# Lightning attention and a leaky-ReLU MLP on one core: a new order of units, conversions and loads, and five constants of the planner

## The chip, the core and the metric

The kernel runs on one core of a Trainium2 chip. The metric is the device time of one execution in microseconds (us), lower is better. The kernel before took 597.89 us, the median of three runs (597.32 to 598.83). A separate execution was profiled; its times are the ones in the profile.

The core has five engines with queues of their own, which run side by side and wait for each other by semaphores: TensorE (PE: matrix products and transposes), VectorE (DVE), ScalarE (ACT), GpSimd (POOL) and SyncE (SP), which here only issues transfers between DRAM and the on-chip memory. Each engine executes its queue strictly in the order in which it was written. So an order of the program is an order of five queues.

## The reference

Attention with decay over four batches, eight heads, 768 positions and 64 features, in blocks of 64, with a running state per head; then a two-layer MLP on the 3072 tokens with weights in double precision.

```python
for b in range(nb):                                  # nb = 12 blocks of 64
    intra = np.einsum('bhic,bhjc->bhij', qb, kb) * Dmask[None]
    intra = np.einsum('bhij,bhjd->bhid', intra, vb)
    inter = np.einsum('bhid,bhde->bhie', qb * lam_pow[None], kv_state)
    out[:, :, sl] = intra + inter
    kb_dec = kb * rev_pow[None]
    kv_state = lam_block[None, :, None, None] * kv_state + np.einsum('bhsd,bhse->bhde', kb_dec, vb)
...
x = np.ascontiguousarray(attn_out.transpose(0, 2, 1, 3)).reshape(B * S, H * D)   # [3072, 512]
h = x @ w_in                                         # [512, 2048], float64
g = np.maximum(0.01 * h, h)
return (g @ w_out).astype(np.float32)                # [2048, 512], float64
```

## The kernel before

**Precision.** Every operand of the two large products is held as three parts, h, l and m, made from a float32 value: h is a rounded copy (ACT), l the remainder against h, m a combination of both (DVE). A product is three matmuls, one for each part, that PE adds up in PSUM. So each operand costs one ACT and two DVE instructions before PE can use it, and they come in that order: h, l, m.

**Tiles.** The 3072 tokens are 24 chunks of 128; four chunks are a group of 512 tokens, so there are six groups, 0 to 5. The 2048 columns of the first product are eight pairs (0 to 7) of 256 columns.

**The up stage, to about 345 us.** A round `r c` does the attention of chunk c and ends with the three parts of x for that chunk (L533 xh on ACT, L534 xl on DVE, then xm). In its middle PE must not go on before a copy of two columns, L517, has read the result of the first half; the planner puts that copy on DVE or on ACT. `up(g, p)` is the first product of group g with pair p: for each half of the columns, four steps of PE (h, l, an ACT pass over the bank at L786, m), and an ACT evacuation with the leaky ReLU at L791. Three PSUM banks, b10, b11 and b2, are used in turn. The result goes to DRAM, plain (`G`) or as sums and differences of its quarters (`BB`, made by `sums` on DVE). `up(1, 5, 0, 3)` is the first three chunks of a group and `up(1, 5, 3, 4)` the last one. `ORDER` lists in which order the pairs come in groups 2 to 4; group 5 takes them from 0 to 7.

**Conversions.** `wi p` loads pair p of the first weight matrix as float64 (L611), splits it into float32 with bit operations on ACT (L614, L616, L618) and DVE (L620, L621), and then makes its parts: the head wh on ACT (L627) or DVE (L629), as the planner chooses, wl on DVE (L632), wm on DVE (L647). `wo p h` converts half a pair of the second matrix and stores it in DRAM. `wp p` (`w_out_parts`) loads it again and makes its three parts in place of the first matrix's: L627 or L629, L632, then L640 (DVE) and L642 (ACT). `ws p` (`w_sums`) makes the sums of quarters of a pair that the Strassen-like units need: a load, four DVE subtractions or additions, and parts as before. `wq p` (`w_apart`, its head L699) does this for pairs 4 and 5 and sends the parts to DRAM; `wd` (`fetches`) fetches them back.

**The down stage, from about 345 us.** Three parts, in the order 0, 2, 1; part pr covers groups 2 pr and 2 pr + 1. Pairs below `NSP = [2, 6, 4]` are multiplied by a Strassen scheme with seven units t = 1 to 7 for each two pairs: `s(t, u)`, 12 matmuls of 128x512 (L909). The other pairs are plain units `n(p, gi)`, 24 matmuls each; the last of a part, written `l`, also turns its results (`turn_out`, DVE L1003) and stores them (`store_out`). Each unit is made ready by `unit`:

```python
add("DMA", UNIT_DMA, go, keys, wr("m"))      # SP: load of 512 KB into part m of a ring slot
add("ACT", 1.05, head, kg, wr("h"))          # L882: h
add("DVE", 1.25, low, kg + [f"rh{j}"], wr("l"))              # L885: l
add("DVE", 1.25, middle, [f"rh{j}", f"rl{j}"], [f"rm{j}"])   # L889: m
```

There are five ring slots, taken in turn in the order in which the units are written, so the load of a unit waits until PE has finished the unit five places before. Where a needed block was not stored, the load is of two blocks (L899) and DVE subtracts them first (L901). The results gather in four pairs of banks, X, Z, Y and V. `copy Z X` and `copy Y Z` (`copy_banks`, L1022, two ACT copies) and `add Y V` and `add V Z` (`add_banks`, L1027 on ACT, L1028 on DVE) move them on at set points; the units write X, V, Z, X, Z, Y, Z for t = 1, 5, 6, 2, 7, 3, 4. The kernel ends with `ending`, two plain units in pieces with their stores.

**What sets the order.** `seq` is a list of such steps, written out by hand. Each step's instructions are given to `Plan` with a length, what they read and write, and a rank: their place in `seq`, less a lead. `emit` then plays the five engines forward with these lengths: again and again the operation that can start first is taken, and among equals the one with the lowest rank. The lengths (`UNIT_DMA = 1.7` for a unit's load, for instance) are the planner's own. They decide nothing but the order of the five queues. `LEAD` (8 places; `LEAD0` for part 0) is the lead of a unit's load, head, l and m, and of copies and additions between banks; `WPR` and `WSR` shift `wp` and `ws` behind their place. After a store that ACT issues, an entry of length 0.55 without an instruction stands in the planner's DMA queue.

Of the kernel before, what the change touches and what calls it, by code (L numbers as in the profile page):

```python
# [166 lines left out]
def kernel(  # L167
# [21 lines left out]
    NG = NCH // GC  # L189
# [13 lines left out]
    NS, NS0 = 4, 2  # L203
    NSP = [2, 6, 4]
    WS0, WS1 = 1, 2
    LEAD = 8.0
    TURN_B = 2
    HOLD, WPR, WSR, LEAD0 = 0.0, 4.0, 2.0, 8.0
    WSLACK = 5.0
    DV = 10  # L210
    QSL = 1.0
    RUNS = {10: (-8.0, 0.8), 12: (4.0, 0.0)}
    C4 = P // 4
    UNIT_DMA, UNIT_SLACK = 1.7, -0.5
    HALF = (slice(0, D), slice(D, 2 * D))
    assert NCB % TURN == 0 and D == 64 and KO == HP == 4 and SEQ % C == 0 and NCH % GC == 0 and d_model == T == 512 and NP % 4 == 0

# [19 lines left out]
    X = [[sb([P, KO, T], f"x{x}{i}", F32R) for x in "hlm"] for i in range(2)]  # L237
# [54 lines left out]
    add = plan.add  # L292
# [713 lines left out]
    def store_out(pr, gi, m, cs, queues):  # L1006
        t0, n, w = (2 * pr + m) * T + gi * HT, HT // C4, len(cs) * C4

        def store(a, q):
            c0 = a * P + cs[0] * C4  # L1010
            q.dma_start(out=out[t0:t0 + HT, c0:c0 + w].rearrange("(b i) j -> i b j", i=C4),
                        in_=otile[a * C4:(a + 1) * C4, m * n:(m + 1) * n, cs[0]:cs[-1] + 1, :].rearrange("i b c j -> i b (c j)"))

        for a, x in enumerate(queues):
            e, q = {"S": ("DMA", nc.sync), "A": ("ACT", nc.scalar)}[x]
            add(e, 0.5, lambda a=a, q=q: store(a, q), [f"o{c}{m}" for c in cs], [f"out{pr}{gi}{m}{a}{cs[0]}"], rank=6.0 if len(cs) == 4 else -1.5)
            if x == "A":
                add("DMA", 0.55, lambda: None, [f"o{c}{m}" for c in cs] + [f"out{pr}{gi}{m}{a}{cs[0]}"], [], rank=6.0 if len(cs) == 4 else -1.5)

    def copy_banks(d, s):  # L1020
        for i in range(2):
            add("ACT", 0.6, lambda i=i: nc.scalar.copy(acc[d][i], acc[s][i]), [ACC[s][i]], [ACC[d][i]], rank=-LEAD)  # L1022

    def add_banks(d, s):
        for i in range(2):
# [3 lines left out]

    seq = [  # L1030
# [5 lines left out]
    nxt, n_out, begin = 3 * GC, 0, len(seq)  # L1036
    ORDER = [2, 1, 4, 3, 0, 5, 7, 6]
    steps = [(g, p) for g in range(2, NG) for p in (ORDER if g < NG - 1 else range(NP))]

    def key_of(g, p):  # L1040
# [16 lines left out]
    for pr, before in ((0, None), (2, 0), (1, 2)):  # L1057
        def s(t, u):
            return "s", pr, t, u

        def n(p, gi, r=pr):
            return ("n", r, p, gi) if p < NP - 1 else ("l", r, p, gi, (0, 1, 2, 3) if gi == 0 else (2, 3, 0, 1))

        late = [n(p, 1, before) for p in range(NS, NP)] if pr else []
        if pr:
            if pr == 2:
                seq += [
                    s(1, 0), s(1, 1), ("copy", "Z", "X"), late[2], late[0], s(6, 1), late[1], ("wq", 4), late[3], s(6, 0),
                    ("copy", "Y", "Z"), s(5, 0), s(5, 1), s(7, 1), ("add", "Y", "V"), s(7, 0), ("add", "V", "Z"), s(2, 1),
                    n(4, 0), s(2, 0), n(6, 0), s(4, 1), n(5, 0), s(4, 0), s(3, 1), s(3, 0), n(7, 0), ("wq", 5)]  # L1070
            else:
                seq += [
                    late[1], late[0], s(1, 0), s(1, 2), s(1, 1), ("wd", 0), late[2], ("copy", "Z", "X"), s(2, 0), s(6, 2),
                    late[3], s(2, 1), ("wd", 2), s(5, 0), s(5, 1), s(6, 0), s(6, 1), ("copy", "Y", "Z"), s(5, 2), s(7, 0),
                    s(2, 2), s(7, 2), ("wd", 1), s(7, 1), ("add", "Y", "V"), ("add", "V", "Z"), s(3, 2), s(4, 0), s(4, 2),
                    s(4, 1), n(6, 0), n(7, 0), s(3, 0), s(3, 1)]
        else:
            def put(x, *new):
                i = seq.index(x)
                seq[i:i] = new  # L1080

            put(("up", NG - 1, 4), ("ws", 0))
            put(("up", NG - 1, 5), ("ws", 1))
            put(("up", NG - 1, 7), ("fr",))
            put(("up", NG - 1, 7), s(1, 0), ("copy", "Z", "X"))
            seq += [
                s(6, 0), s(5, 0), ("copy", "Y", "Z"), s(7, 0), ("add", "Y", "V"), ("add", "V", "Z"), n(2, 0), n(2, 1), n(3, 1),
                s(4, 0), n(3, 0), s(2, 0), n(6, 0), n(5, 0), n(4, 0), ("ws", 2), s(3, 0), ("ws", 3), n(7, 0)]
    seq += [n(p, 1) for p in range(NSP[1], NP - 2)] + [("end", 1, 1, NP - 2)]

    freed = False
    for n, x in enumerate(seq):
# [37 lines left out]
        elif x[0] == "s":  # L1130
            strassen(*x[1:], LEAD if x[1] else LEAD0)
        elif x[0] == "n":
# [40 lines left out]
```

## Time and profile before

| what | value |
|---|---|
| three runs | 597.32, 597.89, 598.83 us |
| the profiled execution, its own time | 598.96 us |
| its span, from the first to the last instruction | 597.2 us |
| POOL: rounds' state products and loads, none after some 270 us | 134.8 us busy |
| granted TensorE clock | 9 or more tenths in all 40 slices of the span |
| mean rate of the transfers | 224 GB/s, 133.55 MB |
| load of a Strassen unit (`xm<-b`, 35 of 512 KB) | median 4.3 us from issue to landing |
| load of a plain unit (`xm<-g`, 17 of 512 KB) | median 4.3 us |
| load of half a pair of `w_in`, of `w_out` (16 each, 512 KB) | 5.2 us, 5.0 us |
| head of a unit, L882 on ACT | 51 times, mean 1062 ns |
| l of a unit, L885 on DVE | 51 times, mean 1219 ns |
| m of a unit, L889 on DVE | 52 times, mean 1225 ns |
| pass over a bank, L786 on ACT | 97 times, mean 582 ns |

The page counts an engine as busy while one of its instructions runs. The line of a group of instructions names the line of the kernel, the engine, the operation and its tiles (out<-in), how many there are, the busy time and the mean of one, and behind the last bar the idle time just before them with what ended it. The list of waits has, for each engine and place, the engine and the operation that ended the wait, then the time waited, the number of waits, and the longest. The chain of waits is followed back from the last instruction, at each step to what released it. In the timeline an instruction's line has its start, its length, its engine and line, the operation, and in square brackets how long the engine had been idle before it and which instruction ended that.

### The profile page before, as it was taken

To read this page: it belongs to the slowest core of one execution; us is meant where nothing else is said; L and a number is where in the kernel's file an instruction comes from. 1 tells how busy PE (TensorE), PEld (TensorE's weight loads), DVE (VectorE), ACT (ScalarE), POOL (GpSimd) and SP (SyncE) were. 2 spreads that over 40 slices of the span, in tenths; PEclk is the share of its full clock that TensorE was granted. 3 is DMA by queue.
4 is the path that set the end of the run, shared out by engine and by line. 5 is a ranking of instruction groups with operands and counts; after the bars stand their busy time and mean duration, and the time that the engine had idled before them with its cause. 6 is when DMAs were issued, how large, how long until landed. Compare 5 with 4: busy or idle time off the path is not lost.

```text
span 597.2 us, 13439 instructions
## 1 busy us (share of the span) xinstructions
PE 584.0 (98%) x5324; PEld 481.7 (81%) x5324; DVE 433.4 (73%) x596; ACT 306.2 (51%) x478; POOL 134.8 (23%) x170
## 2 busy tenths in 40 slices
PE   7899999999999999999999999999999999999997
PEld 5678888888888888888788878888888888888886
DVE  5899986525677464675269989886698887788972
ACT  4688883445555555565588783433343332335410
POOL 2654494616436436431000000000000000000000
PEclk9999999999999999999999999999999999999999
DMA  8899766978989989997889765534868668869644
GB/s 208 224 292 250 239 175 156 228 206 211 264 240 269 242 268 254 261 294 225 260 265 300 239 201 185 187 124 154 236 200 253 195 218 251 281 201 294 186 121 88
DMA packets 171199, 133.55 MB, mean 224 GB/s; under 512 B 101376, under 2 KB 147200, under 8 KB 171136
## 3 DMA queue, kind: packets, MB, share of 16 engines
q1 hardware_dynamic: 155376, 123.24, 70.8%
q10 hardware_dynamic: 13200, 5.77, 3.7%
q0 software_dynamic: 2560, 3.68, 2.4%
q8 instruction: 42, 0.69, 0.5%
q14 instruction: 21, 0.17, 0.1%
HBM read 85.99 MB, written 46.66 MB: 222 GB/s over the span
## 4 chain that ended last, share of the span: by engine, by line
PE 90%; DVE 5%; DMA 2%; ACT 1%; issue 0%; POOL 0%; SPq 0%
PE b L767 42%; PE po L909 13%; PE b L909 12%; PE psc L909 11%; PE pt L909 4%; PE po L339 3%; PE psc L339 3%; DMA attb<-in_q_dram 2%; DVE w L620 1%; DVE wm L647 1%; DVE w L621 1%; DMA attb<-in_k_dram 1%; PE pt L429 1%; DVE wl L632 0%; PE po L429 0%
## 5 line engine op out<-in xcount | busy, mean ns | idle before, releaser
L767 PE MATMUL b<-xh,wh 128*128 128x512 f32 (+2 forms) x392 | 103.5, 387 | 0.9 <-ACT xh L533 0.8
L767 PE MATMUL b<-xl,wl 128*128 128x512 f32 (+2 forms) x392 | 103.4, 387 | 0.7 <-DVE xl L534 0.6
L767 PE MATMUL b<-xm,wm 128*128 128x512 f32 (+2 forms) x392 | 103.9, 393 | 0.0
L882 ACT ACTIVATE xh<-xm 128x1024 fp32r<-128x1024 f32 x51 | 54.1, 1062 | 82.8 <-DMA xm<-b 50.3
L767 PEld LDWEIGHTS b<-xh,wh 128*128 128x128 f32 x392 | 72.8, 188 | 16.8 <-ACT xh L533 0.9
L767 PEld LDWEIGHTS b<-xl,wl 128*128 128x128 f32 x392 | 72.8, 188 | 15.9 <-DVE xl L534 1.0
L767 PEld LDWEIGHTS b<-xm,wm 128*128 128x128 f32 x392 | 71.3, 188 | 14.8
L786 ACT ACTIVATE b<-b 128x512 f32<-128x512 f32 (+2 forms) x97 | 56.2, 582 | 49.0 <-PE b L767 48.5
L791 ACT ACTIVATE gs<-b 128x512 f32<-128x512 f32 (+2 forms) x97 | 57.1, 593 | 44.0 <-PE b L767 38.2
L885 DVE SCALAR_TENSOR_TENSOR xl<-xm,xh 128x1024 fp32r<-128x1024 f32 x51 | 62.2, 1219 | 16.2 <-ACT xh L882 15.8
L889 DVE SCALAR_TENSOR_TENSOR xm<-xl,xh 128x1024 fp32r<-128x1024 f32 x52 | 63.7, 1225 | 4.0
L478 DVE TENSOR_TENSOR att<-psc,att 128x512 f32<-128x512 f32 x24 | 16.5, 688 | 38.9 <-PE psc L339 38.9
L488 POOL TENSOR_TENSOR att<-att 128x256 f32<-128x256 f32 x40 | 33.9, 847 | 42.2 <-DVE att L485 41.3
L400 POOL DMA_DIRECT2D attb<-in_q_dram x64 | 39.4, 622 | 4.9 <-DVE att L409 4.3
L449 POOL TENSOR_TENSOR att<-att 128x512 f32<-128x512 f32 (+1 forms) x20 | 24.8, 1240 | 53.7 <-PE po L339 18.9
L445 POOL TENSOR_TENSOR attb<-attb,att 128x512 f32<-128x512 f32 (+1 forms) x23 | 27.7, 1202 | 37.4 <-DMA attb<-in_k_dram 16.3
L909 PE MATMUL psc<-xm,wm 128*128 128x512 f32 x80 | 31.2, 391 | 0.8 <-DVE xm L889 0.8
L621 DVE CUSTOM_DVE_ANT_0 w<-w,lows 128x1024 uint16<-128x1024 uint16 x32 | 26.3, 822 | 7.3 <-ACT lows L618 5.9
L909 PE MATMUL psc<-xl,wl 128*128 128x512 f32 x80 | 31.2, 390 | 0.0
L909 PE MATMUL psc<-xh,wh 128*128 128x512 f32 x80 | 31.1, 389 | 0.0
L620 DVE TENSOR_SCALAR w<-w 128x512 int32<-128x512 int32 x32 | 22.1, 692 | 8.7 <-ACT w L614 8.5
L616 ACT ACTIVATE lows<-raws 128x512 uint16<-128x512 uint32 x32 | 25.2, 786 | 1.1 <-DVE w L621 1.1
(189 smaller groups left out, 1102.6 us busy)
## 6 DMA issues: line engine op xcount, KB each, us to landing
xm<-b SPq DMA_DIRECT2D x35, 512.0 KB, 4.3
b<-gs SPq DMA_DIRECT2D x24, 512.0 KB, 3.7
g<-gs SPq DMA_DIRECT2D x23, 512.0 KB, 3.6
xm<-g SPq DMA_DIRECT2D x17, 512.0 KB, 4.3
raws<-in_moe_w_in_dram SPq DMA_DIRECT2D x16, 512.0 KB, 5.2
raws<-in_moe_w_out_dram SPq DMA_DIRECT2D x16, 512.0 KB, 5.0
attb<-in_k_dram SPq DMA_DIRECT2D x48, 128.0 KB, 4.2
attb<-in_v_dram SPq DMA_DIRECT2D x24, 256.0 KB, 4.5
```

What stands on the lines that cost most here:

```text
L339: nc.tensor.matmul(dst[HALF[cols]], lhsT=lhsT[HALF[rows]], rhs=rhs[HALF[rows]], start=start, stop=True, skip_group_check=True)
L400: (move if nm == "k" else carry)(0.55 if nm == "k" else QSL, lambda o=o, z=z, e=nc.sync if nm == "k" else nc.gpsimd: e.dma_start(out=o.rea ...
L488: add("POOL", 0.7, lambda new=new, j=j: nc.gpsimd.tensor_tensor(state[(j + 1) % 4], new, _bc(lam_c, 2, D), op=ALU.mult), [f"st{j % 4}", "f ...
L620: add("DVE", 0.42, lambda: nc.vector.tensor_scalar(d, d, 3, None, op0=ALU.logical_shift_left), [], [key])
L621: add("DVE", 1.0, lambda: nc.vector.tensor_tensor(d, d, low, op=ALU.add), [kl], [key])
L767: nc.tensor.matmul(dst, lhsT=w[z][:, kk * 2 * P + f * P:kk * 2 * P + (f + 1) * P], rhs=x[z][:, kk, toks], start=start and kk == 0, stop=kk ...
L786: add("ACT", ns, lambda b=b: nc.scalar.activation(out=b, in_=b, func=AF.Copy, bias=0.0, scale=S + 1.0), [], [kb], rank=-1.5)
L791: add("ACT", t, lambda o=o, x=s_: nc.scalar.activation(out=o, in_=x, func=AF.Prelu, bias=0.0, scale=(1.0 + 1.0 / S) / (WS * U), alpha=0.01 ...
L882: nc.scalar.activation(out=ring[j][0], in_=g(), func=AF.Copy, bias=0.0, scale=NEAR)
L885: nc.vector.scalar_tensor_tensor(ring[j][1], g(), 1.0, ring[j][0].bitcast(F32), op0=ALU.mult, op1=ALU.subtract)
L889: nc.vector.scalar_tensor_tensor(m, l.bitcast(F32), -S, h.bitcast(F32), op0=ALU.mult, op1=ALU.add)
L909: nc.tensor.matmul(dst, lhsT=lhs(z), rhs=ring[j][z][:, col:col + n], start=first and z == 0, stop=z == 2, skip_group_check=True)
```

## The change

The operations stay as they are: the same loads, products and stores are written, with the same lengths and tiles, but for two small choices between DVE and ACT that the planner makes (one more instruction on ACT, one fewer on DVE). What is new is their order, by four kinds of edits.

- Constants: `LEAD` 8 to 12, `WPR` 4 to 3, `LEAD0` 8 to 4, `UNIT_DMA` 1.7 to 1.85, and the entry behind ACT's stores 0.55 to 0.45.
- The head of `seq`, from its third row: which pairs are multiplied with groups 0 and 1, where the rounds 6 to 11 stand between them, and when the conversions 3, 4, 7, 0 and 1 come. The first chunks of `up(1, 5)` move behind `up(0, 4)`, and `r 7` stands ahead of `wi 4`.
- `ORDER` for groups 2 to 4 becomes 1, 6, 0, 3, 2, 5, 7, 4.
- The three parts of the down stage. In part 0 the sums `ws 0` and `ws 1` are put before `up(5, 1)` and `up(5, 3)`, the first Strassen unit and the copy behind it before `up(5, 5)`, unit s(5,0) before s(6,0), and n(6,0) is the first plain unit in place of n(2,0). In the other two parts the plain units that are left from the part before (`late`), the Strassen units and the copies and additions stand in another order. In part 1, in PE's queue as the planner writes it, unit l(7,1) (`late[3]`, four pieces of six matmuls) stood before the change with its first piece behind s(1,2), s(1,1), n(6,1) and s(2,0) and the rest behind s(6,2); now its first two pieces stand behind s(1,2), s(1,1) and n(4,1) and the other two behind s(6,2) and s(6,0). Its ring slot is that of s(1,2) in both.

```diff
--- before.py
+++ after.py
@@ -203,15 +203,15 @@
     NS, NS0 = 4, 2
     NSP = [2, 6, 4]
     WS0, WS1 = 1, 2
-    LEAD = 8.0
+    LEAD = 12.0
     TURN_B = 2
-    HOLD, WPR, WSR, LEAD0 = 0.0, 4.0, 2.0, 8.0
+    HOLD, WPR, WSR, LEAD0 = 0.0, 3.0, 2.0, 4.0
     WSLACK = 5.0
     DV = 10
     QSL = 1.0
     RUNS = {10: (-8.0, 0.8), 12: (4.0, 0.0)}
     C4 = P // 4
-    UNIT_DMA, UNIT_SLACK = 1.7, -0.5
+    UNIT_DMA, UNIT_SLACK = 1.85, -0.5
     HALF = (slice(0, D), slice(D, 2 * D))
     assert NCB % TURN == 0 and D == 64 and KO == HP == 4 and SEQ % C == 0 and NCH % GC == 0 and d_model == T == 512 and NP % 4 == 0
 
@@ -1015,7 +1015,7 @@
             e, q = {"S": ("DMA", nc.sync), "A": ("ACT", nc.scalar)}[x]
             add(e, 0.5, lambda a=a, q=q: store(a, q), [f"o{c}{m}" for c in cs], [f"out{pr}{gi}{m}{a}{cs[0]}"], rank=6.0 if len(cs) == 4 else -1.5)
             if x == "A":
-                add("DMA", 0.55, lambda: None, [f"o{c}{m}" for c in cs] + [f"out{pr}{gi}{m}{a}{cs[0]}"], [], rank=6.0 if len(cs) == 4 else -1.5)
+                add("DMA", 0.45, lambda: None, [f"o{c}{m}" for c in cs] + [f"out{pr}{gi}{m}{a}{cs[0]}"], [], rank=6.0 if len(cs) == 4 else -1.5)
 
     def copy_banks(d, s):
         for i in range(2):
@@ -1029,12 +1029,12 @@
 
     seq = [
            ("a", 0), ("a", 1), ("a", 2), ("a", 3), ("wi", 5), ("b", 4), ("up", 0, 5), ("wi", 2), ("wi", 6), ("r", 4), ("r", 5),
-           ("up", 0, 2), ("up", 0, 6), ("wi", 3), ("up", 0, 3), ("r", 6), ("wi", 4), ("up", 1, 5, 0, 3), ("wi", 7),
-           ("up", 0, 4), ("r", 7), ("up", 0, 7), ("wi", 0), ("up", 1, 3), ("wi", 1), ("up", 0, 1), ("ls",), ("up", 0, 0),
-           ("lt",), ("up", 1, 0), ("r", 8), ("r", 9), ("up", 1, 7), ("up", 1, 4), ("up", 1, 6), ("r", 10), ("r", 11),
-           ("up", 1, 2), ("up", 1, 1), ("up", 1, 5, 3, 4)]
+           ("up", 0, 2), ("wi", 3), ("r", 6), ("up", 0, 6), ("up", 0, 3), ("r", 7), ("wi", 4), ("up", 0, 4), ("wi", 7),
+           ("up", 1, 5, 0, 3), ("up", 1, 4), ("wi", 0), ("wi", 1), ("ls",), ("up", 0, 7), ("up", 0, 0), ("up", 0, 1), ("lt",),
+           ("up", 1, 7), ("r", 8), ("r", 9), ("up", 1, 0), ("up", 1, 3), ("r", 10), ("up", 1, 6), ("r", 11),
+           ("up", 1, 5, 3, 4), ("up", 1, 1), ("up", 1, 2)]
     nxt, n_out, begin = 3 * GC, 0, len(seq)
-    ORDER = [2, 1, 4, 3, 0, 5, 7, 6]
+    ORDER = [1, 6, 0, 3, 2, 5, 7, 4]
     steps = [(g, p) for g in range(2, NG) for p in (ORDER if g < NG - 1 else range(NP))]
 
     def key_of(g, p):
@@ -1065,27 +1065,27 @@
         if pr:
             if pr == 2:
                 seq += [
-                    s(1, 0), s(1, 1), ("copy", "Z", "X"), late[2], late[0], s(6, 1), late[1], ("wq", 4), late[3], s(6, 0),
-                    ("copy", "Y", "Z"), s(5, 0), s(5, 1), s(7, 1), ("add", "Y", "V"), s(7, 0), ("add", "V", "Z"), s(2, 1),
-                    n(4, 0), s(2, 0), n(6, 0), s(4, 1), n(5, 0), s(4, 0), s(3, 1), s(3, 0), n(7, 0), ("wq", 5)]
+                    s(1, 0), late[0], late[1], s(1, 1), ("copy", "Z", "X"), late[2], ("wq", 4), late[3], s(6, 0), s(5, 0),
+                    s(6, 1), s(5, 1), ("copy", "Y", "Z"), s(7, 0), s(7, 1), ("add", "Y", "V"), ("add", "V", "Z"), s(3, 0),
+                    n(4, 0), s(2, 0), n(6, 0), s(4, 1), n(5, 0), s(3, 1), s(4, 0), s(2, 1), n(7, 0), ("wq", 5)]
             else:
                 seq += [
-                    late[1], late[0], s(1, 0), s(1, 2), s(1, 1), ("wd", 0), late[2], ("copy", "Z", "X"), s(2, 0), s(6, 2),
-                    late[3], s(2, 1), ("wd", 2), s(5, 0), s(5, 1), s(6, 0), s(6, 1), ("copy", "Y", "Z"), s(5, 2), s(7, 0),
-                    s(2, 2), s(7, 2), ("wd", 1), s(7, 1), ("add", "Y", "V"), ("add", "V", "Z"), s(3, 2), s(4, 0), s(4, 2),
-                    s(4, 1), n(6, 0), n(7, 0), s(3, 0), s(3, 1)]
+                    late[1], s(1, 0), late[2], s(1, 2), s(1, 1), late[0], ("wd", 0), ("copy", "Z", "X"), s(6, 2), s(6, 0),
+                    ("wd", 2), late[3], s(6, 1), s(5, 0), ("copy", "Y", "Z"), s(5, 2), s(5, 1), ("add", "Y", "V"), s(7, 2),
+                    ("wd", 1), s(7, 0), s(2, 0), s(2, 2), s(2, 1), s(7, 1), s(3, 1), ("add", "V", "Z"), s(4, 0), s(4, 1),
+                    s(4, 2), n(6, 0), n(7, 0), s(3, 0), s(3, 2)]
         else:
             def put(x, *new):
                 i = seq.index(x)
                 seq[i:i] = new
 
-            put(("up", NG - 1, 4), ("ws", 0))
-            put(("up", NG - 1, 5), ("ws", 1))
+            put(("up", NG - 1, 1), ("ws", 0))
+            put(("up", NG - 1, 3), ("ws", 1))
             put(("up", NG - 1, 7), ("fr",))
-            put(("up", NG - 1, 7), s(1, 0), ("copy", "Z", "X"))
+            put(("up", NG - 1, 5), s(1, 0), ("copy", "Z", "X"))
             seq += [
-                s(6, 0), s(5, 0), ("copy", "Y", "Z"), s(7, 0), ("add", "Y", "V"), ("add", "V", "Z"), n(2, 0), n(2, 1), n(3, 1),
-                s(4, 0), n(3, 0), s(2, 0), n(6, 0), n(5, 0), n(4, 0), ("ws", 2), s(3, 0), ("ws", 3), n(7, 0)]
+                s(5, 0), s(6, 0), ("copy", "Y", "Z"), s(7, 0), ("add", "Y", "V"), ("add", "V", "Z"), n(6, 0), n(5, 0), n(2, 0),
+                s(4, 0), n(3, 0), n(2, 1), s(2, 0), n(3, 1), s(3, 0), n(4, 0), n(7, 0), ("ws", 2), ("ws", 3)]
     seq += [n(p, 1) for p in range(NSP[1], NP - 2)] + [("end", 1, 1, NP - 2)]
 
     freed = False
```

`late` is `[n(4, 1), n(5, 1), n(6, 1), l(7, 1)]` of the part before, `put(x, ...)` inserts steps ahead of step x, and ("end", 1, 1, 6) is the call of `ending`.

## The prediction

> **What bounds the kernel now.** I read the engines' busy times first, then TensorE's own waits, then the places of those waits in the order of time.
>
> ```profile
> span 597.2 us, 13439 instructions
> ...
> PE 584.0 (98%) x5324; PEld 481.7 (81%) x5324; DVE 433.4 (73%) x596; ACT 306.2 (51%) x478; POOL 134.8 (23%) x170
> ...
> PE 90%; DVE 5%; DMA 2%; ACT 1%; issue 0%; POOL 0%; SPq 0%
> ```
>
> TensorE (PE) is busy for 98% and makes 90% of the chain. An edit of order alone leaves its 3822 issued matmuls and transposes as they are, and the 30 fillers (L286) stand in the same places in both orders, so the change can only take away or add waits of PE. These are PE's waits from 62 us on, where the two orders part (up to 62 us all five queues agree, apart from two evacuations and one small copy):
>
> ```profile
> PE psc L909 <- DVE xm L889: 0.8, 1, 0.8
> PE b L767 <- DVE xl L534: 0.6, 1, 0.6
> PE po L339 <- DVE att L517: 0.3, 1, 0.3
> PE po L339 <- ACT att L517: 0.3, 1, 0.3
> ```
>
> That is 2.0 us in all. The chain around the largest one shows that it is longer than its 0.8:
>
> ```profile
> 353.15 0.98 ACT wm L642
> 354.13 0.96 ACT w L1027 x2
> 355.09 0.97 ACT xh L882
> 356.06 0.02 issue
> 356.08 1.24 DVE xl L885
> 357.32 0.02 issue
> 357.34 1.24 DVE xm L889
> 358.58 0.04 issue
> 358.62 1.21 PE psc L909 x4
> ```
>
> The first product of unit n(2,0) starts at 356.93; its third, due two products (2 x 0.227) later at 357.38, starts at 358.62: 1.24 us are lost. So PE's losses after 62 us come to 0.64 + 0.34 + 0.28 + 1.24 = 2.50 us. That is the most that the change can win; what it can lose has no such bound.
>
> **The change, part by part.** Unit lengths below are from the timeline of PE: a product of 128x512 every 0.227 us, so an s unit (12) 2.72 and an n unit (24) 5.44; a block of four in the up stage 0.907. A place in the new order is the old place of a common neighbour plus such lengths.
>
> *First units (seq, up to unit r 7).* The old order puts up(1,5) on three chunks behind up(0,3), and its second block waits:
>
> ```profile
> 65.89 0.97 PE L767 MATMUL b<-xl,wl 128*128 128x384 f32 x4 [0.64 <-DVE xl L534]
> ...
> 77.23 0.46 PE L339 MATMUL po<-att 64*64 64x64 f32 x16 [0.34 <-DVE att L517]
> ```
>
> DVE was late with xl there because it made wh of pair 4 first (L629, 62.97 to 64.63). In the new order up(0,4) comes first; its wh moves to ACT (L627, 1.06 in its rows), and a two-column copy (L517) moves from ACT to DVE, behind an L620 that ended at 62.10. That copy releases the last products of chunk 6: it ended at 61.93 and would now end at 62.10 + 0.15 = 62.25. PE took up those products at about 62.1, so 0.15 us are added. Then: L621 ends at 62.25 + 0.69 = 62.94, wh on ACT at 62.94 + 1.06 = 64.0, wl (L632) at 64.0 + 0.05 + 1.22 = 65.27. PE starts xh of up(0,4) at 64.38 + 0.15 = 64.53 and wants wl at 65.44: no wait. With the 1.39 that L632 took at 55.22, beside POOL, it would be 65.44 too; I add 0.1 for the uncertainty. Both sides: 0 if all fits, 0.64 if the same tightness returns.
>
> The second wait (0.34) came from the same small copy behind L620 (75.82 to 77.10). In the new order r 7 comes 4 us earlier (69.9), and ahead of the copy stand wm of pair 4 and four conversions of pair 7: 68.5 + 0.85 + 0.69 + 0.42 + 0.69 = 71.1, while PE reaches the point at 69.9 + 0.9 + 0.7 = 71.5. No wait; if I am wrong, 0.34. Sum of this part: -0.64 - 0.34 + 0.15 + 0.1 = -0.73.
>
> The Trainium skill, "GPSIMD Engine Reference", section "Specifications", says that GpSimd shares its SBUF interfaces with VectorE and that they contend when a VectorE instruction has two SBUF inputs. L632 has two, and POOL's state product (L488) would run beside it at 64.1; the rows differ (1.22 beside POOL at 66.80, 1.39 at 55.22), and what POOL lost is clearer (1.54 against 0.62 alone). By the rule alone wl could be late by some tenths, and the sum would be -0.6 in place of -0.73.
>
> *Order of the up units, 78 to 325 us.* ORDER and seq change which pair is next, not how much. PE had one wait there (0.28 at 295, before a copy on ACT that stays). The rounds r 9 to r 23 fall within 1.3 us of their old places, so their loads have the same time. Cover: ACT 10 to 12 us and DVE 8 to 14 of every 20. A bank that is evacuated one instruction late would cost one L786, 0.58. I take 0.
>
> *Turn from up to down, 325 to 365 us.* Now s(1,0) stands before up(5,5), 5.5 us earlier, s(5,0) before s(6,0), and the weight sums of pair 1 ahead of three conversions. DVE is busy 18.8 of 20 us here and ACT 15.6. Laying the new DVE queue end to end from 296.5 (conversions L632, L640 1.23 each, sums 0.42, unit steps 1.22) I get s(5,0) ready at 338.7 for its start at 347.7, s(6,0) at 344.4 for 351.3 and s(7,0) at 349.4 for 354.0. The thinnest cover is ACT's evacuation of the banks of up(5,6) and up(5,7): 0.4 to 0.9 us. I cost these moves at 0; without cover each costs its overshoot, at most the one head (L882, 1.05) that now stands ahead of an evacuation.
>
> What remains is the wait of the first n unit, now n(6,0). Its head waits on ACT for two bank copies, that can start only when the banks of s(6,0) are written. In the old order the two copies before the head (L1027) began as s(5,0) ended. Same chain: from the end of s(6,0) (354.03) minus 0.15, copies 0.94, head 1.06, DVE 2 x 1.25 = 358.4. PE is there after s(7,0), 354.03 + 2.72, and wants the third product at 357.2: 1.2 late, as before (1.24). So this, the largest wait, is kept. Both sides: 0 (all 1.24 won) if ACT gets the head in before the copies' end; 2.3 if wm of pair 7 (1.06 on ACT) slips behind the copies.
>
> *Down stage, parts 0 and 2.* The order of n units changes; they give slack (5.44 of PE against 2.45 of DVE each). The run of s units after the second l unit grows from six to seven; with two bank copies, four turn_outs (0.7) and w_apart's 4 x 0.42 + 2.45 placed earlier, the thinnest unit, s(6,1), is ready 0.9 us ahead of PE (the old run's thinnest had 1.8). Cost 0.
>
> *Down stage, part 1.* Each unit's load waits for a ring slot, that is for the PE end of the unit five places before in the order of loads.
>
> ```profile
> 508.30 0.53 SPq L879 DMA_DIRECT2D raws<-g  x1
> ...
> 514.71 1.22 DVE L885 SCALAR_TENSOR_TENSOR raws<-raws 128x1024 fp32r<-128x1024 f32 x1 [0.39 <-ACT raws L882]
> 516.04 1.23 DVE L889 SCALAR_TENSOR_TENSOR raws<-raws 128x1024 fp32r<-128x1024 f32 x1
> ```
>
> This is unit l(7,1): slot free as s(1,2) ends at 508.10, load landed at 513.54 (5.24), head 1.06, ready at 517.26, 9.16 after the slot. In the old order 10.88 us of PE (s, n, s) lie between and PE comes at 518.98. In the new one only s(1,1) and n(4,1), 8.16, as PE takes half of l(7,1) before s(6,2). Its third product is due 8.16 + 0.45 = 8.61 after the slot: 0.55 late with this landing, 0.4 early with the 4.3 that is the median of these loads. I take +0.2 (a landing of 4.85, between the two). Behind it the run of s units has more room than before (1.6 us at the thinnest, against 0.49 for s(4,2)), which wins nothing, as there was no wait. The last units and stores are the same.
>
> The constants (LEAD, WPR, LEAD0, UNIT_DMA, 0.45) only rank the queues that are counted above. One 0.15 copy moves to ACT in the balance of instructions.
>
> Sum: -0.73 - 0.04 + 0.2 = -0.6 on the profiled execution, 598.96 (a span of 597.2 and 1.76 around it). That one ran 1.07 above the median of the runs, 597.89; carried over, 597.3.
>
> **Rivals.** (a) *All waits go.* The head of n(6,0) gets in ahead, and l(7,1) is in time: -0.98 + 0.25 - 1.24 = -1.97, 595.9. For it: the order of both is new. Against: the copies depend on s(6,0), which runs right before.
> (b) *The load of l(7,1) is late; slower.* Place: 516 us, slot 4. Price: each 0.1 of landing beyond 4.69 costs PE 0.1; beyond 5.4 it eats the 0.77 won, and the kernel is slower. The longest landings of 512 KB here are 6.9 (issue 354.79, landed 361.65; and 487.86, landed 494.85 at 7.0): 2.3 us lost, 597.89 - 0.77 + 2.3 = 599.4; beyond that more. For it: the fetches and stores (DMA 0.89 of its 16 engines at 500 to 520) run beside it. Against: 5.24 was measured at this very place.
> The Trainium skill, "DMA: Bandwidth & Descriptors", section "Latency and other measured facts", puts HBM access at 0.2 us on average and 2 us at high load. By that page, as an estimate, the median 4.3 could become 6.1, and the time 598.5; landings of 4.3 to 7.0 in this trace agree.
> (c) *Nothing is moved that PE feels*: the early waits return in another place (0.64, 0.34), 597.9 to 598.1. For it: DVE is 93% busy from 60 to 80 us.
>
> **How the numbers follow.** A measurement of this kernel can tell about 0.3% (1.8 us: 596.1 and 599.7). Forecast 0.42, (a) 0.17, (b) 0.27, (c) 0.14. Forecast and (c) lie within 0.3%. Of (a) 0.14 lie below 596.1: the rest keeps a part of the waits. Of (b) I put 0.22 above 599.7, since a landing like the longest leaves only 0.3 to that mark, and a unit that is late also holds ACT's queue, in which its head stands. So faster 0.15, same 0.62, slower 0.23 (0.01 each for what no case holds). The range from 595.7 (2.5 less than the median, less 0.3) to 600.6 (the bound of (b) and one lost head more) leaves out some 2 in 10. The forecast's own range is 596.5 to 598.3.
>
> **What would show it.** Right: no wait at L534 near 66 us nor at L517 near 72; a wait of about 1.2 on xm (L889) of the first n unit near 357; l(7,1) with at most 0.5 near 516; no other PE wait. Wrong: any wait of PE over 0.5 between 78 and 345 us, or in the s runs; a first n unit without a wait (a); more than 1 us at l(7,1) (b).

## The result, and the profile after

| | median | lowest to highest | runs |
|---|---|---|---|
| before | 598.24 us | 597.25 to 599.56 | 12 |
| changed | 599.58 us | 598.50 to 601.95 | 12 |

The ratio is 1.0025 (95% interval 1.0013 to 1.0036): the changed kernel is slower by about 1.5 us. Its profiled execution took 600.06 us, with a span of 598.2. From its page, the lines that answer to those shown of before (span, busy times, the chain of waits by engine):

```profile
span 598.2 us, 13441 instructions
...
PE 584.6 (98%) x5324; PEld 482.3 (81%) x5324; DVE 428.5 (72%) x595; ACT 306.8 (51%) x479; POOL 135.2 (23%) x170
...
PE 87%; DVE 7%; DMA 4%; issue 1%; ACT 1%; POOL 0%; DVEq 0%; ACTq 0%
```

PE still has the same work, 5324 matmul records, but DVE and transfers now have 11% of the chain in place of 7%. PE's waits from 62 us on (engine and place, what ended the wait, then us, number, longest):

```profile
PE po L909 <- ACT b L1022: 1.2, 1, 1.2
PE po L909 <- DVE xm L889: 0.8, 1, 0.8
PE psc L909 <- DVE xm L889: 0.8, 2, 0.5
PE b L909 <- DVE raws L889: 0.3, 1, 0.3
PE po L339 <- ACT att L517: 0.3, 1, 0.3
```

The waits near 66 and 77 us are gone. The wait of the first plain unit is shorter than before (0.30 in place of 0.76 us idle), and four waits are new. The timeline of PE says where these five are (start, length, and in brackets the idle time before):

```profile
353.11 0.50 PE L909 MATMUL po<-xh,att 128*128 128x512 f32 x1 [1.21 <-ACT b L1022]
356.92 0.50 PE L909 MATMUL psc<-xm,wm 128*128 128x512 f32 x1 [0.30 <-DVE xm L889]
515.64 0.50 PE L909 MATMUL b<-raws,wm 128*128 128x512 f32 x1 [0.29 <-DVE raws L889]
541.52 0.50 PE L909 MATMUL po<-xm,att 128*128 128x512 f32 x1 [0.83 <-DVE xm L889]
544.99 0.50 PE L909 MATMUL psc<-xm,wm 128*128 128x512 f32 x1 [0.47 <-DVE xm L889]
```

In order these are s(7,0) and n(6,0) of part 0, l(7,1), and s(7,0) and s(2,0) of part 1. The second is the first plain unit.

Idle time alone is too small a measure, since PE also loses time right behind a wait: after the product at 353.11 the next one started 0.34 us later, where 0.23 is usual. So I took each step of PE in its order, from its start to the start of the next, and subtracted the median length of that kind of step over the twelve profiled executions of this study. Summed by stage, this is the time lost, in us. The up stage runs here from up(0,2) near 37 us to up(5,4) near 320, the turn and part 0 from there to the first piece of l(7,0), part 2 to the first unit of part 1, and part 1 to `ending`.

| kernel | up stage | turn, part 0 | part 2 | part 1 |
|---|---|---|---|---|
| before | 7.73 | 1.43 | 0.16 | 0.23 |
| changed | 6.11 | 2.16 | 0.28 | 2.93 |

So 1.6 us are won in the up stage, 0.7 lost at the turn, 0.1 in part 2 and 2.7 in part 1: 1.9 lost net. Ahead of up(0,2), where the order is the same, these two executions differ by 0.84 in favour of the changed one (over all twelve: by up to 3.3), so their spans differ by 1.0 only.

### The profile page after: what moved, and what is told of

It reads as the page before. It is cut to its first block, busy times and chain, and to the rows that moved or that the text cites. A ratio compares the mean times of both kernels' runs of the same rounds, so it can differ in the third digit from the quotient of the medians.

```text
span 598.2 us, 13441 instructions
## 1 busy us (share of the span) xinstructions
PE 584.6 (98%) x5324; PEld 482.3 (81%) x5324; DVE 428.5 (72%) x595; ACT 306.8 (51%) x479; POOL 135.2 (23%) x170
## 4 chain that ended last, share of the span: by engine, by line
PE 87%; DVE 7%; DMA 4%; issue 1%; ACT 1%; POOL 0%; DVEq 0%; ACTq 0%
PE b L767 42%; PE po L909 12%; PE b L909 11%; PE psc L909 10%; PE po L339 4%; PE pt L909 3%; PE psc L339 3%; DVE w L621 1%; DMA xm<-b 1%; DMA raws<-g 1%; DVE w L620 1%; DMA xm<-g 1%; DVE wl L632 1%; DMA out_dram<-gs 1%; PE pt L429 1%
## 5 line engine op out<-in xcount | busy, mean ns | idle before, releaser
L786 ACT ACTIVATE b<-b 128x512 f32<-128x512 f32 (+2 forms) x97 | 56.1, 581 | 51.5 <-PE b L767 51.3
L791 ACT ACTIVATE gs<-b 128x512 f32<-128x512 f32 (+2 forms) x97 | 57.0, 592 | 40.8 <-PE b L767 37.4
L488 POOL TENSOR_TENSOR att<-att 128x256 f32<-128x256 f32 x40 | 35.2, 879 | 34.2 <-DVE att L485 33.4
L909 PE MATMUL psc<-xm,wm 128*128 128x512 f32 x84 | 32.9, 392 | 0.8 <-DVE xm L889 0.8
L909 PE MATMUL psc<-xh,wh 128*128 128x512 f32 x84 | 32.8, 390 | 0.0
L909 PE MATMUL psc<-xl,wl 128*128 128x512 f32 x84 | 32.7, 389 | 0.0
L909 PE MATMUL b<-xh,wh 128*128 128x512 f32 x68 | 26.5, 389 | 0.0
```

The source lines that it names most:

```text
L488: add("POOL", 0.7, lambda new=new, j=j: nc.gpsimd.tensor_tensor(state[(j + 1) % 4], new, _bc(lam_c, 2, D), op=ALU.mult), [f"st{j % 4}", "f ...
L786: add("ACT", ns, lambda b=b: nc.scalar.activation(out=b, in_=b, func=AF.Copy, bias=0.0, scale=S + 1.0), [], [kb], rank=-1.5)
L791: add("ACT", t, lambda o=o, x=s_: nc.scalar.activation(out=o, in_=x, func=AF.Prelu, bias=0.0, scale=(1.0 + 1.0 / S) / (WS * U), alpha=0.01 ...
L909: nc.tensor.matmul(dst, lhsT=lhs(z), rhs=ring[j][z][:, col:col + n], start=first and z == 0, stop=z == 2, skip_group_check=True)
```

## The experiments

The times are medians; the ratios are against runs of the kernel before on the same chip (its medians there: 598.22 for the first four, 597.75 for the next four, 598.41 for the last two).

| run | median | ratio (95% interval) | up stage | turn, part 0 | part 2 | part 1 |
|---|---|---|---|---|---|---|
| e1_early | 596.82 | 0.9970 (0.9960 to 0.9980) | 6.00 | 1.41 | 0.16 | 0.23 |
| e2_swap | 602.39 | 1.0063 (1.0043 to 1.0083) | 5.79 | 4.65 | 0.16 | 1.98 |
| e3_store_late | 598.57 | 1.0000 (0.9989 to 1.0012) | 6.07 | 2.39 | 0.16 | 1.12 |
| e4_part1_old | 597.65 | 0.9984 (0.9972 to 0.9996) | 7.64 | 2.42 | 0.16 | 0.23 |
| e5_head | 603.63 | 1.0094 (1.0076 to 1.0111) | 10.08 | 6.22 | 0.16 | 0.23 |
| e6_const_old | 602.36 | 1.0084 (1.0065 to 1.0103) | 6.95 | 2.59 | 1.27 | 2.97 |
| e7_swap_add | 598.03 | 1.0005 (0.9996 to 1.0015) | 6.49 | 1.32 | 0.16 | 2.17 |
| e8_early_s6 | 595.62 | 0.9969 (0.9957 to 0.9981) | 5.97 | 0.78 | 0.16 | 0.23 |
| e9_pool | 598.44 | 1.0009 (0.9995 to 1.0024) | 6.95 | 2.49 | 0.20 | 0.58 |
| e10_all | 597.40 | 0.9982 (0.9971 to 0.9993) | 6.07 | 1.87 | 0.16 | 1.85 |

The four columns on the right come from one execution each; the 7.64 of e4 holds one wait of 1.0 for which the page names no engine.

### The early lists alone (e1)

The kernel before, with two edits of the change:

```diff
-           ("up", 0, 2), ("up", 0, 6), ("wi", 3), ("up", 0, 3), ("r", 6), ("wi", 4), ("up", 1, 5, 0, 3), ("wi", 7),
+           ("up", 0, 2), ("wi", 3), ("r", 6), ("up", 0, 6), ("up", 0, 3), ("r", 7), ("wi", 4), ("up", 0, 4), ("wi", 7),
...
-    ORDER = [2, 1, 4, 3, 0, 5, 7, 6]
+    ORDER = [1, 6, 0, 3, 2, 5, 7, 4]
```

> The kernel before with the new head of seq and the new ORDER alone; constants and down stage as before. Theory (each loss has its own place): the up stage wins what the two traces differ by between 44 and 327 us, 1.75 us, and the turn and the down stage lose nothing: about 1.7 us faster than before, 0.997, no PE wait at L534 near 66 us nor at L517 near 77, the first plain unit's wait on L889 near 356 still there (1.4 lost). Rival (the up stage's win is only the two waits that the trace names): 1.0 us faster, 0.9984. Rival (the difference of the two traces there is chance of one execution): 1.000.

Measured: 0.997, 1.8 us faster. The early half of the change is worth its full 1.7 us, and down stage and turn are as before. PE's waits of this run from 44 us on; the last two lines are a copy ahead of 62 us and the one near 295 us:

```profile
PE psc L909 <- DVE xm L889: 0.8, 1, 0.8
PE po L339 <- DVE att L517: 0.3, 1, 0.3
PE po L339 <- ACT att L517: 0.3, 1, 0.3
```

The win is larger than the two waits that PE's list named (0.98 us of idle). These are waits of the weight loads (PEld) in the kernel before, from 62 to 130 us; the prediction did not read them. One line, of short waits for nothing that the profile shows, is left out:

```profile
...
PEld b L767 <- DVE xl L534: 1.0, 1, 1.0
PEld b L767 <- DVE wh L629: 0.5, 1, 0.5
PEld po L339 <- DVE att L517: 0.5, 1, 0.5
```

The middle line is a third loss, near 92 us. By steps the three cost PE 0.81, 0.52 and 0.39, together 1.72; none of them is left here.

### One store moved by one place (e3), and the stores on another engine (e9)

Why are s(7,0) and s(2,0) of part 1 late? ACT's timeline in the changed kernel (ACTq is a transfer that ACT issues; its length runs from the first issue to the last):

```profile
532.15 1.06 ACT L882 ACTIVATE raws<-raws 128x1024 fp32r<-128x1024 f32 x1 [1.28 <-DMA raws<-b]
532.18 5.54 ACTq L1011 DMA_DIRECT2D out_dram<-gs  x4
537.82 2.01 ACT L882 ACTIVATE xh<-xm 128x1024 fp32r<-128x1024 f32 x2 [4.60 <-DMA out_dram<-gs]
```

ACT is idle for 4.60 us, although the load of s(7,0) had landed at 534.3. The chain of waits says what for:

```profile
531.92 5.40 DMA xm<-b
537.32 0.02 issue
537.34 4.03 DMA out_dram<-gs
541.38 1.22 DVE xl L885
```

The last of the four stores was issued at 537.34, as soon as another unit's load (that of s(2,0)) had landed at 537.32. The store needs nothing of that load. The program's listing of ACT's queue shows the link. It names, for each instruction, the semaphores that it waits for (Activation and PE are those of the engines, DMAHW0 to DMAHW7 those of transfers):

```
L882  Activation raws<-raws  [waits DMAHW7, Activation]      head of s(7,2)
L1011 DMACopy out_dram<-gs
L1011 DMACopy out_dram<-gs   [waits DMAHW1]
L1011 DMACopy out_dram<-gs   [waits DMAHW3]
L1011 DMACopy out_dram<-gs   [waits DMAHW4]                  the eighth store
L882  Activation xh<-xm      [waits DMAHW2, Activation]      head of s(7,0)
L882  Activation xh<-xm      [waits PE, Activation]          head of s(2,0)
```

The transfers of SP and ACT share eight semaphores, DMAHW0 to DMAHW7, handed out in turn; a transfer that gets one still in use waits until its last user has landed. The eighth store gets DMAHW4, which the load of s(2,0) holds (in e3 that head waits for DMAHW4 itself; here the store ahead of it has already done so). The trace agrees: the load issued at 531.92 and the store issued at 537.34 use one semaphore, which the trace numbers 105. The engine that issues waits, so ACT stands still, and with it the head of s(7,0). Neither `seq` nor the planner's lengths know of this wait.

In the kernel before, ACT issues the same eight stores between 536 and 543 us. The heads beside them waited for their own loads alone, and PE lost nothing there:

```profile
537.17 1.06 ACT L882 ACTIVATE xh<-xm 128x1024 fp32r<-128x1024 f32 x1 [2.53 <-DMA xm<-b]
537.19 1.70 ACTq L1011 DMA_DIRECT2D out_dram<-gs  x3
539.88 1.06 ACT L882 ACTIVATE xh<-xm 128x1024 fp32r<-128x1024 f32 x1 [1.66 <-DMA xm<-b]
```

In e3 only that store changes its place; this is ACT's queue, not the source:

```diff
 L882 Activation raws<-raws
-L1011 DMACopy out_dram<-gs x4
-L882 Activation xh<-xm x2
+L1011 DMACopy out_dram<-gs x3
+L882 Activation xh<-xm
+L1011 DMACopy out_dram<-gs
+L882 Activation xh<-xm
```

> The changed kernel with one instruction moved by one place on ACT: the last store (L1011) of part 2's unit l(7,1) stands behind the head of s(7,0) of part 1 instead of ahead of it. Theory: that store waits for a semaphore that an earlier load of 512 KB still holds, and the head behind it waits with it; without it the head starts when its load lands, some 3.5 us earlier, and PE's 1.24 and 0.76 lost near 540 and 544 us go: 2.0 us faster than the changed kernel, 0.999 of before; l(7,1) still loses 0.6 near 515. Rival (the units there are late because their loads land late and DVE does them one behind the other): no more than 0.3 us changes, 1.002 to 1.003.

Measured: 1.0000, which is 1.5 us faster than the changed kernel where 2.0 were expected. PE's loss at s(7,0) is gone, at s(2,0) 0.26 is left, and part 1 loses 1.12 in place of 2.93. ACT's heads of these two units in e3:

```profile
535.80 1.06 ACT L882 ACTIVATE xh<-xm 128x1024 fp32r<-128x1024 f32 x1 [3.02 <-DMA out_dram<-gs]
...
537.29 1.06 ACT L882 ACTIVATE xh<-xm 128x1024 fp32r<-128x1024 f32 x1 [0.43 <-DMA xm<-b]
```

The first head still stood behind two other stores, which were issued from 534.88 on; its load had landed at 534.69. It started 2.0 us earlier than in the changed kernel, and that was early enough for PE. By the medians about 1.5 us come from one instruction that stood one place too early.

In e9 the eight stores of that unit are issued by POOL:

```diff
-            e, q = {"S": ("DMA", nc.sync), "A": ("ACT", nc.scalar)}[x]
+            e, q = {"S": ("DMA", nc.sync), "A": ("ACT", nc.scalar), "P": ("POOL", nc.gpsimd)}[x]
...
-            store_out(pr, gi, m, range(4), "AAAA")
+            store_out(pr, gi, m, range(4), "PPPP" if (pr, gi) == (2, 1) else "AAAA")
```

> The changed kernel with the eight stores of part 2's unit l(7,1) issued by POOL, which has nothing to do in the down stage, in place of ACT; ACT's other instructions and PE's and DVE's orders stay. Theory: no store stands ahead of a head any more, the heads of s(7,0) and s(2,0) start when their loads land (near 534.3 and 537.3), and both waits of PE near 540 and 544 go: 2.0 us faster than the changed kernel, 0.9988 to 0.9995 of before; the 0.6 at l(7,1) and the 1.2 at s(7,0) of part 0 stay. Rival (the loads are late themselves, or the stores now hold POOL's queue and the banks behind it): 1.002 or more.

Measured: 1.0009 (0.9995 to 1.0024), about 1 us faster than the changed kernel, less than the 2.0 expected. The profile is clear. ACT's timeline at the same place:

```profile
538.11 1.06 ACT L882 ACTIVATE xh<-xm 128x1024 fp32r<-128x1024 f32 x1 [3.21 <-DMA xm<-b]
540.92 1.06 ACT L882 ACTIVATE xh<-xm 128x1024 fp32r<-128x1024 f32 x1 [1.75 <-DMA xm<-b]
```

Each head now waits for its own load, and neither unit costs PE anything: part 1 loses 0.58 in all, of which 0.25 is l(7,1). In the trace the stores from POOL use semaphores of their own (111 to 118). So e9 takes away both the store ahead of the head and the shared semaphore. In e3 the store stays on ACT, but its semaphore changes with its place (to 106).

### The old list in part 1 (e4), and the old constants (e6)

e4 is the changed kernel with the old list of steps for pr = 1 (`late[1], late[0], s(1, 0), s(1, 2), ...`).

> The changed kernel with the old list of steps in part 1. Theory: l(7,1) loses nothing and the stores are no longer ahead of a head that PE waits for, so 2.6 to 2.8 us are won against the changed kernel: 0.998 of before. Rival (part 1 is bound by what comes from part 2, whose list and slots stay new): 0 to 1 us won, 1.001 to 1.0025.

Measured: 0.9984, as expected. Part 1 is back at 0.23; the new list of part 1 is what turns the change from a win into a loss.

e6 is the changed kernel with

```diff
-    LEAD = 12.0
+    LEAD = 8.0
-    HOLD, WPR, WSR, LEAD0 = 0.0, 3.0, 2.0, 4.0
+    HOLD, WPR, WSR, LEAD0 = 0.0, 4.0, 2.0, 8.0
-    UNIT_DMA, UNIT_SLACK = 1.85, -0.5
+    UNIT_DMA, UNIT_SLACK = 1.7, -0.5
-                add("DMA", 0.45, lambda: None, ...)
+                add("DMA", 0.55, lambda: None, ...)
```

> The changed kernel with the five constants of before (8, 4, 8, 1.7, 0.55). With them the planner puts only six of the eight stores of part 2's unit l(7,1) ahead of the head of s(7,0) in ACT's queue, and two of those ahead of the head of s(2,0). Theory: the head of s(7,0) is no longer behind a store whose semaphore a late load holds, so the 2.0 us near 540 shrink to less than 0.8; s(5,0), s(6,0), copy, s(7,0) and l(7,1) still lose 0.7 and 0.6: 0.9995 to 1.001 of before. Rival (the constants only rank, the lists alone cost): 1.0025.

Measured: 1.0084, a miss. The head of s(7,0) was free, but the two stores behind it now held the head of s(2,0). ACT's timeline of e6:

```profile
535.38 1.06 ACT L882 ACTIVATE xh<-xm 128x1024 fp32r<-128x1024 f32 x1 [1.61 <-DMA xm<-b]
535.41 5.50 ACTq L1011 DMA_DIRECT2D out_dram<-gs  x2
541.03 1.06 ACT L882 ACTIVATE xh<-xm 128x1024 fp32r<-128x1024 f32 x1 [4.58 <-PE po L909]
```

The bracket names PE; but the second store was issued only at 540.58, and ACT could not reach the head before. A load issued at 535.51 had landed at 540.56. s(2,0) cost 2.55, and n(4,0) of part 2 another 1.11, waiting for the bank copies (L1027) on ACT. The mechanism was the expected one; that the next head has no more cover than the one spared I had not worked out. The steps show 2.3 us more lost than in the changed kernel, while the ratios differ by 0.0059, about 3.5 us. The granted clock of the six executions fits the rest: the profiled one and one other had a mean of 1.000 and took 601.42 and 601.33, the other four had 0.997 and took 601.97 to 605.44. All twelve of the changed kernel had 0.999 or more. No execution with 0.997 was profiled, so which wait brought the clock down is not shown.

### The two units at the turn (e2, e7)

```diff
-                s(5, 0), s(6, 0), ("copy", "Y", "Z"), s(7, 0), ("add", "Y", "V"), ("add", "V", "Z"), n(6, 0), ...
+                s(6, 0), s(5, 0), ("copy", "Y", "Z"), s(7, 0), ("add", "Y", "V"), ("add", "V", "Z"), n(6, 0), ...
```

> The changed kernel with s(6,0) before s(5,0) again in part 0, all else as changed. Theory: the copies of the Z banks (L1022) again run while PE does s(5,0), so the wait of s(7,0) on them (1.21) goes; the wait of the first plain unit comes back to its old size. The turn loses 1.45 as before in place of 2.17: 0.7 us faster than the changed kernel, 1.0013 of before. Rival (the order of the two is indifferent, the turn is bound by ACT's and DVE's queues): the same lost time in another place, 1.0025 of before.

Measured: 1.0063, by the ratios 2.3 us slower than the changed kernel: a miss. The wait of s(7,0) went as expected, but the planner now put the additions of `add V Z` between the l and the m of n(6,0). DVE and PE in e2:

```profile
354.79 1.23 DVE L885 SCALAR_TENSOR_TENSOR xl<-xm,xh 128x1024 fp32r<-128x1024 f32 x1 [0.27 <-ACT xh L882]
356.45 0.70 DVE L1028 TENSOR_TENSOR b<-b,w 128x512 f32<-128x512 f32 x1 [0.44 <-ACT w L1027]
357.06 0.69 DVE L1028 TENSOR_TENSOR pt<-pt,w 128x512 f32<-128x512 f32 x1
357.66 1.22 DVE L889 SCALAR_TENSOR_TENSOR xm<-xl,xh 128x1024 fp32r<-128x1024 f32 x1
```

```profile
358.93 0.50 PE L909 MATMUL psc<-xm,wm 128*128 128x512 f32 x1 [2.36 <-DVE xm L889]
...
360.97 0.63 PE L909 MATMUL po<-xh,wh 128*128 128x512 f32 x1
361.40 0.63 PE L909 MATMUL po<-xl,wl 128*128 128x512 f32 x1
```

The additions wait for s(7,0) to end on PE, and m waits behind them. PE, due at 356.08, goes on at 358.93 and then runs slowly for 3 us (more on this at the end). e7 is e2 with these two additions one place later on DVE; again this is the queue:

```diff
 L885 TensorScalarPtr xl<-xm,xh
+L889 TensorScalarPtr xm<-xl,xh
 L1028 TensorTensor b<-b,w
 L1028 TensorTensor pt<-pt,w
-L889 TensorScalarPtr xm<-xl,xh
```

> The changed kernel with s(6,0) before s(5,0), and the two additions of add V Z (L1028) moved by one place on DVE, from ahead of the m of n(6,0) (L889) to behind it. Theory: in the run with the swap alone it was these two additions, which wait for s(7,0) to end, that kept m (357.75 instead of 356.0) and PE (2.85 us), and the slower TensorE after that wait cost 1.8 more. Without them m ends at 357.2, PE loses 1.2, its clock stays: 3.4 us faster than the swap alone, 0.7 to 1.0 faster than the changed kernel, 1.0005 to 1.0015 of before. Rival (the swap is slow by the copies or the heads on ACT): 1.005 or more.

Measured: 1.0005, as expected; the turn loses 1.32, about as before the change (1.43). DVE of e7:

```profile
352.54 1.23 DVE L885 SCALAR_TENSOR_TENSOR xl<-xm,xh 128x1024 fp32r<-128x1024 f32 x1 [0.18 <-ACT xh L882]
353.80 1.23 DVE L889 SCALAR_TENSOR_TENSOR xm<-xl,xh 128x1024 fp32r<-128x1024 f32 x1
```

### The head of seq without ORDER (e5)

e5 is e1 without its second edit, so with the old ORDER.

> The kernel before with the new head of seq alone (ORDER, constants and down stage as before). Theory: all that the up stage wins lies in the head, where the traces part by 1.6 of 1.75 us until 125 us: 0.997 of before, like the run with ORDER too. Rival (ORDER has its share): 0.998 to 0.999.

Measured: 1.0094, slower than before by 5.6 us: a miss, though the first 130 us went as expected. Near 248 us up(4,2) waited for L791, which waited for the store of a buffer:

```profile
244.82 5.75 DMA b<-gs
...
250.68 0.60 ACT gs L791
251.28 0.04 issue
251.33 0.95 PE b L767 x2
```

This cost 3.7 us by the steps. At the turn the additions stood between l and m of n(2,0), as in e2, and 6.2 were lost. In both places a part of the loss is PE's clock: it was granted at 0.50 from 251.7 to 255.1 and from 360.9 to 367.7, in and right behind the two waits, and the products of 128x512, else 0.227 apart, stood 0.42 to 0.43 apart. As an estimate, 8 products in the first stretch and 13 in the second, each 0.2 longer, make 1.6 and 2.6 of the 3.7 and 6.2. The two halves of the early edit are not worth the sum of their parts: the planner answered to the old ORDER with a late store more than a hundred microseconds behind the new head.

### A version that beats both (e1, e8), and the repairs together (e10)

```diff
-            put(("up", NG - 1, 7), s(1, 0), ("copy", "Z", "X"))
+            put(("up", NG - 1, 7), s(1, 0), ("copy", "Z", "X"), s(6, 0))
...
-                s(6, 0), s(5, 0), ("copy", "Y", "Z"), s(7, 0), ("add", "Y", "V"), ...
+                s(5, 0), ("copy", "Y", "Z"), s(7, 0), ("add", "Y", "V"), ...
```

> A try for a version that beats both: the kernel before with the new head and ORDER, and s(6,0) of part 0 moved ahead of the last up unit, behind s(1,0) and the copy, so that its ring slot comes free some 6 us earlier and n(2,0), which takes that slot, is ready when PE comes. Theory: the 1.4 us at the first plain unit go: 0.9945 to 0.995 of before. Rival (the copies of Z must now wait for the banks of the last up unit, or a head stands behind them): the wait only moves, 0.997.

Measured: 0.9969, a miss: 0.9945 to 0.995 was expected, and the rival came out. The wait of the first plain unit is gone; from 44 us on PE waits only

```profile
PE b L767 <- ACT b L786: 0.3, 1, 0.3
PE po L339 <- ACT att L517: 0.3, 1, 0.3
```

A half of the 1.4 has moved to the last up unit, whose bank pass L786 is now late. The steps give 0.6 less lost at the turn than in e1 (0.78 against 1.41), but the ratios cannot tell the two apart. Both beat the kernel before and the changed one.

e10 is e7 with e9's edit.

> The changed kernel with the three repairs together: s(6,0) before s(5,0), the two additions behind the m of n(6,0), and the eight stores on POOL. Theory: the repairs concern separate places and add up: 1.0005 of the run with the first two, less the 1.5 us (0.76 and 0.73) that it still lost near 538 and 541: 0.998 of before; l(7,1) still loses 0.5. If the losses that I count are all there are, it comes within 0.001 of the kernel before with the new head and ORDER (0.997). Rival (what is won in one place is lost in the next): 1.000 or more.

Measured: 0.9982, as expected. This execution had a slow landing at l(7,1) (1.21 us lost).

## Why the prediction was wrong

The forecast was 597.3, 0.6 less than the median before; the change made the kernel 1.3 us slower by the medians and 1.5 by the ratio. The step that turned the sign is the cost of 0 for the run of s units in part 1, which lost 2.0 because an output store held ACT's queue. The terms of the sum, one by one:

- **First units, -0.73: right in kind, too small.** Both waits went and none took their place, but the stage won 1.6. What failed here is "PE's losses after 62 us come to 2.50 us. That is the most that the change can win": it counted PE's idle time alone. The weight load that waited near 92 us and the time lost right behind each wait were not in it. The 0.1 added for wl of pair 4 was not needed: L632 took 1.23 there, beside POOL's state product, and ended at 64.46, before PE came to it at 64.62.
- **ORDER, 0: held,** in the sense that nothing was lost between 130 and 320 us. e5 shows that it was not free of effect: the new head with the old ORDER loses 3.7 us there.
- **Turn: "the largest wait, is kept" and cost 0: wrong, 0.7 lost.** I let PE reach n(6,0) "after s(7,0), 354.03 + 2.72". But s(7,0) writes the Z banks, and `copy Y Z` must read them first. With s(6,0) now right before s(7,0), the copies (L1022, 351.99) cannot run under s(5,0) any more, and PE waits 1.21 ahead of s(7,0); it then waits less (0.30) for the m of n(6,0). I had worked out the copies' times for the head behind them, and not for PE. e7 closes this: with s(5,0) between and m ahead of the additions, the turn loses 1.32.
- **l(7,1), +0.2: right in kind, its size set by the landing.** Its load took 5.09 us here and the third product came 0.45 late. Over the seven executions with the new list the landing was 4.70, 4.70, 4.76, 4.96, 5.09, 5.14 and 5.71, and the third product was late by 0.06, 0.07, 0.12, 0.33, 0.45, 0.50 and 1.08: the landing less 4.64, where the prediction had 4.69. Rival (b), a landing beyond 5.4, did not decide here, and was met once in seven.
- **The run of s units behind it, 0 ("more room than before"): wrong, 2.0 lost.** This is the step that decided. I checked loads against ring slots and DVE's steps against PE, and took the stores on ACT as free. ACT's queue is in order; a store that waits for its semaphore holds the heads behind it. In the kernel before the stores stood beside other heads, and none of their waits reached PE. e3, e6 and e9 show it from three sides. The rivals spoke of ACT's queue held by a late unit (b), not of a store.

The signs at the places add up: the early lists 1.8 faster (e1), the list of part 1 2.4 slower (e4 against the changed kernel), the turn 0.7 slower by its steps; 1.3 in sum.

Three readings of the prediction do not come out of the records, and none of them decided. The two traces have 5324 matmul records each, 30 of them fillers; no view of them gives the count of 3822. Of the two longest landings of rival (b), the one from 487.86 is a store (L703); the longest load, 6.9, gives 2.2 in place of 2.3. And 599.4 and one head of 1.06 make 600.5, not 600.6.

The Trainium skill, "DMA: Bandwidth & Descriptors", section "Anatomy of one DMA — SWDGE (gpsimd) path", says that DMA engines do not wait on semaphores: any such wait is on the issuing sequencer, ahead of the dispatch. The trace agrees: ACT, not the transfer, stood still for 4.60 us.

## What to carry to other kernels

In a kernel where PE is busy for 98% and the planner fixes only an order, look for what each queue's next instruction waits for, and count transfers that a compute engine issues among them: an output store ahead of a head is free only while no semaphore is late. List for every moved step whose data it overwrites, not only whose data it needs, and read the waits of the weight loads beside those of PE. Edits that were made together should be measured together: by the ratios e5, which is e1 without one edit, was 7.4 us slower than e1, and e6, which is the changed kernel without its constants, was 3.5 us slower than that.

## What had not been expected of the hardware

After PE's idle 2.36 us in e2 its products of 128x512, else 0.227 apart, stood 0.42 to 0.43 apart from 360.55 to 363.53, which began 1.6 us after PE had gone on; this cost 1.6 us on top of the wait, and the mean granted clock of this run was 0.996. After waits of 1.2 us nothing of the kind is seen. The Trainium skill, "TensorE: Matmul & The Clock Gate", section "Part 1: The HAM clock gate (the "warmup" mystery)", has PE at half rate after an idle window of about 3.4 us: the halved rate agrees with the trace; here an idle time shorter than the window was enough.

In e2 the clock was granted at 0.50 from 360.3 to 363.7 us, and in e5, after PE had stood idle for 2.05 us, from 251.7, 0.4 us after PE had gone on. The same program does not always bring it: two of the six executions of e2 had a mean granted clock of 1.000 and took 600.35 and 601.14, the other four 0.996 or 0.997 and took 602.17 to 604.17.

The start of the kernel scatters more than the change is worth: with the same order of PE's steps, up(0,2) began between 35.4 and 38.8 us in the twelve executions.
